# A fused attention and feed-forward kernel: two more batches of attention output turned by the DMA crossbar, and the last output group in two column halves

**Chip, cores, metric.** One core of one Trainium2 chip. The metric is the device time of one execution in microseconds (us).

## The reference

Block-causal attention over 8 batches, 8 heads, 576 positions, head size 64, then a feed-forward layer with a swish of slope beta on the 4608 rows:

```python
scores = 1/sqrt(64) * q @ k.T                  # (8, 8, 576, 576), keys of later 64-blocks masked
attn = softmax(scores)
x = (attn @ v) as rows (b, s), columns (h, d)  # 4608 x 512
h = x @ w_in                                   # 4608 x 2048
g = h / (1 + exp(-beta * h))
out = g @ w_out                                # 4608 x 512, float32
```

## The kernel before

The kernel is a list of operations that a planner in Python puts in order before the program is built. It imitates the engines and the DMA queue with fixed durations, and the outcome is one fixed order for each engine. In the program that is built each engine has its fixed list, with waits at semaphores between them. TensorE (PE) alternates between attention, in 32 units of two heads of a batch, and the feed-forward layer, in 9 row tiles of 512 rows (`w_in` on L740, `w_out` on L771).

SyncE (SP) only issues DMAs in this kernel. An issue is the time for which one DMA holds the queue; the DMA lands when its data has arrived. The queue issues the loads of q, k and v and all transposes by the DMA crossbar. From batch 2 on the crossbar turns q and k (QKT, one transpose of 2560 columns for two units). The attention output `xq` of a unit has to be turned too, into `xT`: up to batch XB - 1 on PE with a copy (nearly all by VectorE, DVE), from batch XB on by the crossbar:

```python
QB, XB, CAST = 2, 5, "POOL"
...
def pieces(b):                       # where batch b lies in xT, a ring of RX = 2560 columns
    z = []
    for t0, n in ((0, 512), (512, 64)):
        x0 = (S * b + t0) % RX
        m = min(n, RX - x0)
        z.append((t0, m, x0))
        if m < n:
            z.append((t0 + m, n - m, 0))
    return z
...
av = P.op("PE", 30 * 34, fav, deps=..., tiles=[te, Tv, pv, ti, tx], ...)   # values, L653; tx is an xq buffer, of two
...
if b >= XB:
    def fy(g, e, tx=tx, c=c, b=b):
        z = []
        for t0, n, x0 in pieces(b):
            ...                      # i: blocks of xq, m: 128 or the 64 of the last block
            z.append(g.dma_start_transpose(xT[:, c, x0:x0 + n].rearrange("c (t n) -> c t n", n=m), i))   # L685
        return z
    n = len(pieces(b))
    xt.append(P.op("SP", 400 + 300 * n + 700, fy, deps=nrm, tiles=[tx], xfer=1100, prio=-1, ...))
    continue
...                                  # else: five PE transposes (L697), DVE copies them to xT (L707)
```

The numbers in `P.op` are what the planner believes, in ns. The end of each row tile is four groups of 16 matmuls of 512 columns (in parts of four), each scaled by ScalarE (ACT, L782) into one of three `ost` buffers and stored (L788).

The softmax here doesn't subtract the row's maximum and nothing guards it: scores larger than these inputs give would overflow.

Of the kernel before, what the change touches and what calls it, by code (L numbers as in the profile page):

```python
# [4 lines left out]
ACT = mybir.ActivationFunctionType  # L5
ALU = mybir.AluOpType
# [7 lines left out]
DM = 512  # L14
NROWS = B * S
RC = 512
NRC = NROWS // RC
NJ = NF // 128
# [310 lines left out]
def bass_blockwise_causal_attn__then__act_swish_beta_kernel(  # L329
# [10 lines left out]
    with es:  # L340
        def sb(name, shape, dt):
            return es.enter_context(nc.sbuf_tensor(name, shape, dt))

        NQ = 2
        QB, XB, CAST = 2, 5, "POOL"
        NE = 3
        NS = 6
        RX = 5 * RC
# [16 lines left out]
        w_out = sb("w_out", [128, NJ, DM], bf16)  # L365
# [3 lines left out]
        gT = [sb(f"gT{i}", [128, NJ, RC], bf16) for i in range(2)]  # L369
        ost = [sb(f"ost{i}", [128, DM], f32) for i in range(3)]  # L370
        warm = sb("warm", [128, 2], f32)
        PS = es.enter_context(nc.psum_tensor("PS", [128, 8, 512], f32))
# [4 lines left out]
        P = Plan()  # L377
# [4 lines left out]
        def mm(n):  # L382
            return max(n / 2.4 + 3, 55.0)

        def act_t(n, ptr=0):
            return 0.833 * n + 93 + 93 * ptr

        def dve_t(n):
            return (n + 125) / 0.96

        LAG = 2
        def pr(u):
            b, c = divmod(u, NPAIR)
            return u if b < 1 else 10 * u if b < 2 else 994 + 100 * (b - LAG) + 4.9 * c

        def mk(fn):
            return lambda g, e: fn(g)
# [3 lines left out]
            out=identF[:], in_=identF[:], compare_op=ALU.not_equal, fill=1.0, base=0,  # L401
# [3 lines left out]
            out=identB[:], in_=identB[:], compare_op=ALU.not_equal, fill=1.0, base=0,  # L405
# [5 lines left out]
        for i in range(NQ):  # L411
# [3 lines left out]
            o = P.op("POOL", 200, mk(lambda g, i=i: g.memset(Vn[i][:, 4, :, 64:66], 0.0)), prio=-5)  # L415
# [6 lines left out]
        for i in range(NQ, NE):  # L422
# [8 lines left out]
                  deps=[bt, c2], tiles=[tb], lat=400, mode="full", prio=5)  # L431
        bC = P.op("DVE", dve_t(16), lambda g, e: g.tensor_scalar(
            out=beta[:], in0=PS[:, tb.slot, 0:NJ], scalar1=0.5, scalar2=None, op0=ALU.mult), deps=[bT], tiles=[tb])
# [3 lines left out]
        win, wout = [], []  # L437
# [15 lines left out]
        for i in range(NFILL):  # L453
# [10 lines left out]
            n = 215 if i < 16 else 110  # L464
            o = P.op("PE", n, ff, deps=[c2, c4], tiles=[tf], lat=n, mode="full", prio=1e6 + i)
# [6 lines left out]
        for b in range(B):  # L472
            ts, t = P.tile("Vs"), P.tile("V")
            tl[b] = t
            for h0, h1 in ([(0, 4), (4, 8)] if b == 0 else [(0, 8)]):
                vs = []
                for i in range(6):
# [8 lines left out]
                    n = (h1 - h0) / 8 * (1 if i < 4 else 0.25)  # L486
# [4 lines left out]
                n = (h1 - h0) / 8  # L491

                def fw(g, e, ts=ts, t=t, h0=h0, h1=h1):
                    return g.tensor_copy(Vn[t.slot][:, :, h0:h1, 0:64], Vs[ts.slot][:, :, h0:h1, :])  # L494

                o = P.op("POOL", 300 + 2140 * n, fw, deps=[*vs, *ones, *vzero], tiles=[ts, t],
                         prio=4 * b + 0.5 - (38.5 - 5 * (h0 > 0)) * (b < 1))
# [7 lines left out]
        def pieces(b):  # L505
# [8 lines that stand above are left out]
# [4 lines left out]
        for u in range(NU):  # L518
# [8 lines left out]
            if b < QB:  # L527

                turned = []
                for w, (nm, src) in enumerate((("Q", q), ("K", k))):  # L530
# [6 lines left out]
                    o = ld[nm, u] = P.op("SP", 420, fl, tiles=[ts], xfer=1050, prio=u, dma=["d_S", 0, 1])  # L537
                    o.pkt = 80.0

                    def fn(g, e, ts=ts, tn=tn, p=p, w=w):  # L540
# [4 lines left out]
                    o = P.op("POOL" if onp else "DVE", 850 if onp else 750, fn, deps=[o], tiles=[ts, tn],  # L545
                             prio=-40 + 3 * u if onp else -1)

                    def ft(g, e, tn=tn, pt=pt, p=p, w=w):
                        for i in range(6):
# [4 lines left out]
                    o = P.op("PE", 6 * 43, ft, deps=[o, c4], tiles=[tn, pt, tt_], lat=6 * 43 + 170, mode="full",  # L554
                             prio=pr(u))
# [6 lines left out]
            elif p == 0:  # L562

                for w, (nm, src) in enumerate((("Q", q), ("K", k))):
                    ts = P.tile("ST")

                    def fl(g, e, ts=ts, src=src, b=b, c=c):
# [3 lines left out]
                             for i in range(4)]  # L571
# [4 lines left out]
                    o = ld[nm, u] = ld[nm, u + 1] = P.op("SP", 5 * 600, fl, deps=szero, tiles=[ts], xfer=3200, prio=u,  # L576
                                                         dma=["d_S5", 0, 5])
# [17 lines left out]
            for g0 in range(4):  # L595
                ps = P.tile("PP" if g0 < 3 else "P1")

                def fq(g, e, ps=ps, g0=g0, tqk=tqk, p=p):
                    blocks = {0: [(0, 0, 512, 0)], 1: [(1, 128, 576, 0), (0, 512, 576, 448)],
                              2: [(2, 256, 576, 0), (3, 384, 576, 320)], 3: [(4, 512, 576, 0)]}[g0]  # L600
                    for t, q0, q1, off in blocks:
                        m = min(128, 576 - 128 * t)
                        for h in range(2):
# [9 lines left out]
                o = P.op("PE", 220 if g0 < 3 else 60, fq, deps=cps, tiles=[ps, tqk] + [te] * (b > 0),  # L613
                         lat=(220 if g0 < 3 else 60) + 200, mode="row", prio=pr(u) + .1 + .1*(g0 >= 2))
                if g0 < 3:
# [3 lines left out]
                    x = P.op("ACT", act_t(1024), fe, deps=[o], tiles=[ps, te], lat=act_t(1024) + 93, prio=0)  # L619
# [7 lines left out]
                else:  # L627
                    def fe(g, e, ps=ps, te=te):
                        return g.activation(E4[te.slot][:], PS[:, ps.slot, 0:64], ACT.Exp, scale=0.125)  # L629
                    x = P.op("ACT", act_t(64), fe, deps=[o], tiles=[ps, te], lat=act_t(64) + 93, prio=0)  # L630
# [17 lines left out]
            def fav(g, e, te=te, pv=pv, Tv=Tv, c=c):  # L648
                for h in range(2):
                    for i in range(5):  # L650
# [7 lines left out]
                      lat=30 * 34 + 180, mode="full", prio=pr(u)+.4 + 5 * (b < 1))  # L658
# [8 lines left out]
            r = P.op("DVE", 150, fr, deps=[av], tiles=[pv, ti], prio=0)  # L667
# [9 lines left out]
            if b >= XB:  # L677
# [10 lines left out]
                n = len(pieces(b))  # L688
# [40 lines left out]
        for r in range(NRC):  # L729
            row = RC * r  # L730
            b0, b1 = row // S, (row + RC - 1) // S
            xd = [xt[4 * b + c] for b in range(b0, b1 + 1) for c in range(4)]
            tg = P.tile("gT")
            gs, hs = [], []
            for j in range(NJ):
                ph, tt = P.tile("P1"), P.tile("th")

                def fh(g, e, ph=ph, j=j, row=row):
                    for c in range(4):
                        z = g.matmul(PS[:, ph.slot, :], w_in[:, c, 128 * j:128 * j + 128], xT[:, c, row % RX:row % RX + RC],  # L740
                                     start=(c == 0), stop=(c == 3))
                    return z

                o = P.op("PE", 4 * mm(512), fh, deps=xd + [win[j // 4]], tiles=[ph, tg], lat=4 * mm(512) + 170,
                         mode="full", prio=1000 + 100 * r + j)

                hs.append(o)

                def fs(g, e, ph=ph, tt=tt, j=j):
                    return g.activation(th[tt.slot][:], PS[:, ph.slot, :], ACT.Tanh, scale=beta[:, j:j + 1])  # L750
                a = P.op("ACT", act_t(512, 1), fs, deps=[o, bC], tiles=[ph, tt], lat=act_t(512, 1) + 93, prio=0)

                def fg(g, e, ph=ph, tt=tt, tg=tg, j=j):
                    return g.scalar_tensor_tensor(out=gT[tg.slot][:, j, :], in0=th[tt.slot][:], scalar=1.0,  # L754
                                                  in1=PS[:, ph.slot, :], op0=ALU.add, op1=ALU.mult)
                gs.append(P.op("DVE", dve_t(512), fg, deps=[a], tiles=[ph, tt, tg], prio=0))

            for b in range(B):
                if any((S * b + a) // RC - RX // RC == r for a in (0, S - 1)):
                    for c in range(4):  # L760
                        xt[4 * b + c].deps += hs
            for w in range(4):
                po, to = P.tile("P1"), P.tile("ost")


                parts = [(4 * a, 4 * a + 4) for a in range(4)]
                o = None
                for j0, j1 in parts:
                    def fo(g, e, po=po, tg=tg, w=w, j0=j0, j1=j1):
                        for j in range(j0, j1):  # L770
                            z = g.matmul(PS[:, po.slot, :], gT[tg.slot][:, j, 128 * w:128 * w + 128], w_out[:, j, :],  # L771
                                         start=(j == 0), stop=(j == NJ - 1))
                        return z

                    n = j1 - j0
                    o = P.op("PE", n * mm(512), fo, deps=gs[j0:j1] + wout[j0 // 4:(j1 + 3) // 4] + ([o] if o else []),
                             tiles=[po, tg], lat=n * mm(512) + 170, mode="full",
                             prio=1000 + 100 * r + 16 + (w + 0.01 * j0 if r or w > 2 else 0.01 * j0 + 0.001 * w))

                def fv2(g, e, po=po, to=to):  # L780
                    if e == "ACT":
                        return g.activation(ost[to.slot][:], PS[:, po.slot, :], ACT.Copy, scale=0.5)  # L782
                    return g.tensor_scalar(out=ost[to.slot][:], in0=PS[:, po.slot, :], scalar1=0.5, scalar2=None,
                                           op0=ALU.mult)
                x = P.op("ACT", 600, fv2, deps=[o], tiles=[po, to], lat=680, prio=0)

                def fd(g, e, to=to, row=row, w=w):
                    return [g.dma_start(out[row + 128 * w:row + 128 * w + 128, :], ost[to.slot][:])]  # L788
                P.op("ACT", 500, fd, deps=[x], tiles=[to], xfer=900, dma=["d_ost", to], prio=-1)

        P.schedule()
# [69 lines left out]
```

## Time and profile before

| | before |
|---|---|
| time, median of 4 runs | 354.8 us (353.98 to 356.67) |
| span of the profiled run | 353.9 us |
| PE, end of the last matmul | 350.5 us |
| PE transposes of xq (L697) / xT transposes on SP (L685) | 100 / 24 |
| PE wait for QKT landings | 0.5 us |

The profiled run is one execution, and its span is about 1.8 us under its time. The prediction starts from 355.6 us, the median of three runs. SP's share is not on the page, since issues are not counted as busy.

### The profile page before, as it was taken

How to read it: one execution, taken by the hardware profiler on the slowest of the kernel's cores; microseconds unless marked ns; L12 is line 12 of the kernel's file. 1: busy time of each engine (PE TensorE's matmuls, PEld its weight loads, DVE VectorE, ACT ScalarE, POOL GpSimd, SP SyncE). 2: the span in 40 equal slices, each digit the busy share in tenths (PEclk: the TensorE clock that was granted, in tenths of full speed). 3: DMA queues.
4: the chain of work that ended last, by engine and by line, in shares of the span. 5: the costliest groups of instructions: out<-in, count | busy, mean ns of one | idle time of the engine just before them, and what ended most of it. 6: DMA issues, size and time to landing. Idle time of an engine off the chain costs nothing.

```text
span 353.9 us, 6788 instructions
## 1 busy us (share of the span) xinstructions
PE 337.4 (95%) x2734; PEld 168.4 (48%) x2779; DVE 163.6 (46%) x367; ACT 212.0 (60%) x314; POOL 76.3 (22%) x105
## 2 busy tenths in 40 slices
PE   7897999999999999999999999999999999999996
PEld 4473455444455445545544445444444444444442
DVE  4665785055434664227821474137704703802810
ACT  2945973269376797189772976298616715814821
POOL 6476071214044053053013310500000000000000
PEclk9998999999999999999999999999999999999999
DMA  7999999999999999998489986861111011011002
GB/s 209 188 243 231 185 186 200 238 212 193 209 251 204 211 212 203 225 250 167 85 189 166 220 175 143 199 138 36 32 63 59 0 61 59 0 61 59 1 31 89
DMA packets 146528, 52.05 MB, mean 147 GB/s; under 512 B 134704, under 2 KB 141888, under 8 KB 146496
## 3 DMA queue, kind: packets, MB, share of 16 engines
q1 hardware_dynamic: 137088, 37.97, 53.8%
q10 hardware_dynamic: 5184, 9.44, 8.1%
q0 software_dynamic: 4224, 4.19, 7.3%
q8 instruction: 22, 0.36, 0.4%
q14 instruction: 10, 0.08, 0.1%
HBM read 36.71 MB, written 9.44 MB: 130 GB/s over the span
## 4 chain that ended last, share of the span: by engine, by line
PE 75%; SPq 7%; DMA 6%; ACT 5%; issue 3%; DVE 2%; POOL 1%; ACTq 0%; POOLq 0%
PE PS L771 31%; PE PS L740 30%; PE PS L609 6%; PE PS L653 5%; DMA w_in<-in_moe_w_in_dram 3%; ACT E L617 2%; DMA QKT<-QKn 2%; ACT th L750 2%; SPq L480 2%; SPq L685 2%; PE PS L697 2%; SPq L483 2%; DVE gT L754 2%; SPq L569 1%; DMA Vs<-in_v_dram 1%
## 5 line engine op out<-in xcount | busy, mean ns | idle before, releaser
L740 PE MATMUL PS<-xT,w_in 128*128 128x512 bf16 x552 | 129.8, 381 | 5.5 <-DMA w_in<-in_moe_w_in_dram 2.3
L754 DVE SCALAR_TENSOR_TENSOR gT<-th,PS 128x512 bf16<-128x512 f32 x144 | 97.5, 684 | 79.2 <-ACT th L750 78.5
L771 PE MATMUL PS<-w_out,gT 128*128 128x512 bf16 x555 | 128.6, 379 | 2.4 <-issue 1.9
L617 ACT ACTIVATE E<-PS 128x1024 bf16<-128x1024 f32 x96 | 95.9, 1041 | 29.9 <-PE PS L609 29.7
L750 ACT ACTIVATE th<-PS,beta 128x512 f32<-128x512 f32 x144 | 98.1, 706 | 26.3 <-PE PS L740 25.5
L740 PEld LDWEIGHTS PS<-xT,w_in 128*128 128x128 bf16 x576 | 53.1, 98 | 67.3 <-issue 5.1
L771 PEld LDWEIGHTS PS<-w_out,gT 128*128 128x128 bf16 x576 | 53.3, 98 | 64.3 <-issue 4.1
L782 ACT ACTIVATE ost<-PS 128x512 f32<-128x512 f32 x36 | 21.7, 603 | 75.4 <-PE PS L771 75.4
L580 POOL CAST QKn<-ST 128x640 bf16<-128x640 f32 x48 | 34.7, 722 | 55.6 <-DMA ST<-in_k_dram 29.6
L609 PE MATMUL PS<-QKT 64*64 64x64 bf16 (+5 forms) x384 | 38.8, 283 | 1.1 <-DMA QKT<-QKn 0.5
L653 PEld LDWEIGHTS PS<-Vn,E 128*128 128x128 bf16 x960 | 32.6, 97 | 6.2 <-ACT E L629 0.3
L494 POOL CAST Vn<-Vs 128x2560 bf16<-128x2560 f32 (+1 forms) x9 | 18.8, 2088 | 77.2 <-DMA Vs<-in_v_dram 69.5
L653 PE MATMUL PS<-Vn,E 128*128 128x65 bf16 x960 | 33.9, 193 | 0.0
L623 DVE MEMSET E<- 64x64 uint32 x64 | 7.2, 112 | 49.7 <-ACT E L617 48.3
L609 PEld LDWEIGHTS PS<-QKT 64*128 64x128 bf16 (+1 forms) x384 | 13.3, 96 | 28.9 <-issue 10.9
L672 DVE TENSOR_TENSOR xq<-PS,inv 128x640 bf16<-128x640 f32 x32 | 26.3, 823 | 0.8
L707 DVE COPY xT<-PS 128x64 bf16<-128x64 bf16 (+2 forms) x40 | 9.6, 287 | 9.6 <-PE PS L697 9.5
L558 DVE COPY QKT<-PS 128x576 bf16<-128x576 bf16 x16 | 12.0, 756 | 4.5 <-PE PS L550 4.2
L665 DVE RECIPROCAL inv<-PS 128x10 f32<-128x10 f32 x32 | 7.0, 218 | 14.1 <-PE PS L653 13.9
L541 POOL CAST QKn<-ST 96x768 bf16<-96x768 f32 x14 | 11.8, 845 | 6.4 <-DMA ST<-in_k_dram 3.4
L625 DVE MEMSET E<- 64x128 uint32 x32 | 5.3, 165 | 13.6 <-ACT E L617 12.3
L697 PE MATMUL PS<-identB,xq 128*128 128x128 bf16 (+1 forms) x100 | 10.5, 216 | 0.5 <-DVE xq L672 0.3
(33 smaller groups left out, 57.9 us busy)
## 6 DMA issues: line engine op xcount, KB each, us to landing
out_dram<-ost ACTq DMA_DIRECT2D x36, 256.0 KB, 2.5
Vs<-in_v_dram SPq DMA_DIRECT2D x28, 256.0 KB, 4.1
ST<-in_q_dram SPq DMA_DIRECT2D x48, 128.0 KB, 3.2
ST<-in_k_dram SPq DMA_DIRECT2D x48, 128.0 KB, 3.2
ST<-in_q_dram SPq DMA_DIRECT2D x8, 288.0 KB, 6.2
ST<-in_k_dram SPq DMA_DIRECT2D x8, 288.0 KB, 6.8
w_in<-in_moe_w_in_dram POOLq DMA_DIRECT2D x4, 512.0 KB, 14.8
w_out<-in_moe_w_out_dram POOLq DMA_DIRECT2D x4, 512.0 KB, 10.6
```

The costliest lines, as they stand in the source:

```text
L494: return g.tensor_copy(Vn[t.slot][:, :, h0:h1, 0:64], Vs[ts.slot][:, :, h0:h1, :])
L580: return g.tensor_copy(QKn[tn.slot][:].rearrange("p a w n -> p (a w n)")[:, 640 * (2 * a + w):][:, 0:640] .rearrange("p (t h d) -> p t h d ...
L609: z = g.matmul(o, QKT[tqk.slot][r, p, 1, 128 * t:128 * t + m], QKT[tqk.slot][r, p, 0, q0:q1])
L617: return g.activation(E3[te.slot][:, g0, :, :], PS[:, ps.slot:ps.slot + 2, :], ACT.Exp, scale=0.125)
L653: z = g.matmul(o, eblk(te, t, i, h), Vn[Tv.slot][:, t, 2 * c + h, 0:65], start=(t == 0), stop=(t == i))
L672: return g.tensor_tensor(xq[tx.slot][:].rearrange("p i (h d) -> p h i d", h=2), both(pv, 0, 64), x, ALU.mult)
L697: z = g.transpose(PSb[:, px.slot, 128 * i:128 * i + r], xq[tx.slot][0:r, i, :], identB[0:r, 0:r])
L740: z = g.matmul(PS[:, ph.slot, :], w_in[:, c, 128 * j:128 * j + 128], xT[:, c, row % RX:row % RX + RC], start=(c == 0), stop=(c == 3))
L750: return g.activation(th[tt.slot][:], PS[:, ph.slot, :], ACT.Tanh, scale=beta[:, j:j + 1])
L754: return g.scalar_tensor_tensor(out=gT[tg.slot][:, j, :], in0=th[tt.slot][:], scalar=1.0, in1=PS[:, ph.slot, :], op0=ALU.add, op1=ALU.mult)
L771: z = g.matmul(PS[:, po.slot, :], gT[tg.slot][:, j, 128 * w:128 * w + 128], w_out[:, j, :], start=(j == 0), stop=(j == NJ - 1))
L782: return g.activation(ost[to.slot][:], PS[:, po.slot, :], ACT.Copy, scale=0.5)
```

## The change

The intent is to take 40 transposes off PE, the engine that is busy all the time, and to shorten the end: the last of the 36 groups becomes two of 256 columns, so that the last scaling and the last store are of half the size.

```diff
-        QB, XB, CAST = 2, 5, "POOL"
+        QB, XB, CAST = 2, 3, "POOL"
...
-            for w in range(4):
+            for w, d0, d1 in [(w, 0, DM) for w in range(4 if r < NRC - 1 else 3)] + (
+                    [] if r < NRC - 1 else [(3, 0, DM // 2), (3, DM // 2, DM)]):
...
-                            z = g.matmul(PS[:, po.slot, :], gT[tg.slot][:, j, 128 * w:128 * w + 128], w_out[:, j, :],
+                            z = g.matmul(PS[:, po.slot, 0:d1 - d0], gT[tg.slot][:, j, 128 * w:128 * w + 128],
+                                         w_out[:, j, d0:d1], start=(j == 0), stop=(j == NJ - 1))
...                                  # durations, scaling and store in the same way with d0 and d1
```

More of the change, by code (lines that the diff above doesn't have):

```diff
@@ L768, in bass_blockwise_causal_attn__then__act_swish_beta_kernel, with fo @@
                 for j0, j1 in parts:
-                    def fo(g, e, po=po, tg=tg, w=w, j0=j0, j1=j1):
+                    def fo(g, e, po=po, tg=tg, w=w, j0=j0, j1=j1, d0=d0, d1=d1):
                         for j in range(j0, j1):
-                            z = g.matmul(PS[:, po.slot, :], gT[tg.slot][:, j, 128 * w:128 * w + 128], w_out[:, j, :],
-                                         start=(j == 0), stop=(j == NJ - 1))
-                        return z
-                    n = j1 - j0
@@ L776, in bass_blockwise_causal_attn__then__act_swish_beta_kernel @@
-                    o = P.op("PE", n * mm(512), fo, deps=gs[j0:j1] + wout[j0 // 4:(j1 + 3) // 4] + ([o] if o else []),
-                             tiles=[po, tg], lat=n * mm(512) + 170, mode="full",
-                             prio=1000 + 100 * r + 16 + (w + 0.01 * j0 if r or w > 2 else 0.01 * j0 + 0.001 * w))
-                def fv2(g, e, po=po, to=to):
-                    if e == "ACT":
-                        return g.activation(ost[to.slot][:], PS[:, po.slot, :], ACT.Copy, scale=0.5)
-                    return g.tensor_scalar(out=ost[to.slot][:], in0=PS[:, po.slot, :], scalar1=0.5, scalar2=None,
-                                           op0=ALU.mult)
@@ L785, in bass_blockwise_causal_attn__then__act_swish_beta_kernel @@
-                x = P.op("ACT", 600, fv2, deps=[o], tiles=[po, to], lat=680, prio=0)
-                def fd(g, e, to=to, row=row, w=w):
-                    return [g.dma_start(out[row + 128 * w:row + 128 * w + 128, :], ost[to.slot][:])]
+                            z = g.matmul(PS[:, po.slot, 0:d1 - d0], gT[tg.slot][:, j, 128 * w:128 * w + 128],
+                                         w_out[:, j, d0:d1], start=(j == 0), stop=(j == NJ - 1))
+                        return z
+                    n = (j1 - j0) * mm(d1 - d0)
@@ new lines, in bass_blockwise_causal_attn__then__act_swish_beta_kernel, with fv2 @@
+                    o = P.op("PE", n, fo, deps=gs[j0:j1] + wout[j0 // 4:(j1 + 3) // 4] + ([o] if o else []),
+                             tiles=[po, tg], lat=n + 170, mode="full",
+                             prio=1000 + 100 * r + 16 + (w + 0.01 * j0 + 0.3 * (d0 > 0) if r or w > 2 else
+                                                         0.01 * j0 + 0.001 * w))
+                def fv2(g, e, po=po, to=to, n=d1 - d0):
+                    if e == "ACT":
+                        return g.activation(ost[to.slot][:, 0:n], PS[:, po.slot, 0:n], ACT.Copy, scale=0.5)
+                    return g.tensor_scalar(out=ost[to.slot][:, 0:n], in0=PS[:, po.slot, 0:n], scalar1=0.5,
+                                           scalar2=None, op0=ALU.mult)
@@ L789, in bass_blockwise_causal_attn__then__act_swish_beta_kernel, with fd @@
+                x = P.op("ACT", act_t(d1 - d0) + 80, fv2, deps=[o], tiles=[po, to], lat=act_t(d1 - d0) + 160, prio=0)
+                def fd(g, e, to=to, row=row, w=w, d0=d0, d1=d1):
+                    return [g.dma_start(out[row + 128 * w:row + 128 * w + 128, d0:d1], ost[to.slot][:, 0:d1 - d0])]
                 P.op("ACT", 500, fd, deps=[x], tiles=[to], xfer=900, dma=["d_ost", to], prio=-1)
```

## The prediction

> **What bounds the kernel now.** I read the page first: engine shares, the row of slices, the chain that ended last.
>
> ```profile
> PE 337.4 (95%) x2734; PEld 168.4 (48%) x2779; DVE 163.6 (46%) x367; ACT 212.0 (60%) x314; POOL 76.3 (22%) x105
> ...
> PE   7897999999999999999999999999999999999996
> ...
> DMA  7999999999999999998489986861111011011002
> ...
> PE 75%; SPq 7%; DMA 6%; ACT 5%; issue 3%; DVE 2%; POOL 1%; ACTq 0%; POOLq 0%
> ```
>
> PE is busy in every slice, so the matmul stream in its fixed program order sets the time, and what shortens that stream is worth its full length. But the DMA row is full until about 155 us, and 7% of the chain is SP's queue, which issues all loads and all crossbar transposes. So next I read SP's own timeline. An excerpt (start, length, line, operation, tile):
>
> ```profile
> 197.56 2.31 SPq L569 DMA_DIRECT2D ST<-in_k_dram  x4
> 199.91 0.60 SPq L572 DMA_DIRECT2D ST<-in_k_dram  x1
> 200.56 4.11 SPq L587 DMA_TRANSPOSE QKT<-QKn  x1
> 204.72 1.21 SPq L480 DMA_DIRECT2D Vs<-in_v_dram  x2
> 205.97 3.00 SPq L685 DMA_TRANSPOSE xT<-xq  x2
> 209.01 3.14 SPq L587 DMA_TRANSPOSE QKT<-QKn  x1
> 212.19 2.77 SPq L685 DMA_TRANSPOSE xT<-xq  x2
> ```
>
> Each record begins some 0.05 us after the last ended. From 91 to 233 us SP pauses noticeably only once, from 165.5 to 169.5, where it waits for the first attention output of batch 5. It is as full as PE, and the page's engine shares do not show it, because issues are not counted as busy there. The third view, the chain in order of time, shows how close this comes to PE:
>
> ```profile
> 230.24 8.18 DMA QKT<-QKn
> 238.42 0.14 issue
> 238.56 0.22 PE PS L609 x2
> ```
>
> The last of twelve QKT transposes (batch 7, second pair of head pairs) lands at 238.4, and PE begins to use it at 238.56. The list of waits gives 0.5 us of PE time for it, the only wait of the kind. I set each QKT landing from 91 us on beside the first scores matmul of its pair: they are early by 5.8, 7.5, 8.4, 8.7, 9.3, 10.9, 11.5, 2.5, 15.6 and 0.1 us. So SP keeps up with PE, and no more.
>
> **What the Trainium skill says.** "Perfetto Trace Analysis", section "What 'DMA-bound' means", lists as one form that the issuing engine's track is solid with DMA slices, which are descriptor generation. That is SP here. Its section "Per-instruction lifecycle" (the part on HWDGE) says that such a record starts when the semaphores are satisfied and does not hold the data movement; the trace agrees: an xT transpose is 1.23 us long and lands 2.5 us after its issue. "DMA: Bandwidth & Descriptors", section "Issuing engines are not separate DMA queues", calls the issue time usually small beside the transfer; this trace differs, since an xT transpose holds the queue for half its time to landing. "TensorE: Matmul & The Clock Gate", section "Back-to-back issue gap", gives 518 cycles for 512 columns and 262 for 256; the trace has four L740 matmuls in 0.86 us, 216 ns each, and agrees on the first. Nothing in the trace has an isolated stream of 256 warm columns; I take 108 ns, half of 216.
>
> **The change part by part.** Part one concerns batches 3 and 4, eight units (a unit is two heads of a batch).
>
> ```profile
> L697 PE MATMUL PS<-identB,xq 128*128 128x128 bf16 (+1 forms) x100 | 10.5, 216 | 0.5 <-DVE xq L672 0.3
> L707 DVE COPY xT<-PS 128x64 bf16<-128x64 bf16 (+2 forms) x40 | 9.6, 287 | 9.6 <-PE PS L697 9.5
> ...
> xT<-xq SPq DMA_TRANSPOSE x24, 2.5
> ```
>
> Removed from PE: five transposes a unit, 40 of the 100. By the start of the next operation in PE's timeline the eight groups took 0.45, 0.45, 0.33, 0.34, 0.46, 0.45, 0.34 and 0.34 us, 3.2 us together, all on the path. Removed from DVE: copies of 0.52 us (batch 3) and 0.59 us (batch 4), 4.4 us, beside an engine with half its time idle: counted as nothing.
>
> Added to SP: batch 3 lies in xT in two pieces, batch 4 in three because the ring of 2560 columns wraps in it, so 4 x 2 + 4 x 3 = 20 transposes at 1.23 us, 24.6 us, all between 112 and about 175 us and all ahead of the last QKT. Not all becomes delay. The pause of 4.0 us disappears. And issues between 91 and 165.5 us are longer than the shortest of their line: summed over 48 q and k issues, 12 short ones, 15 of v and 6 QKT transposes, 11.9 us over the minimum. I take that for pressure from the full DMA engines, of which a slower stream of loads gives back between nothing and all; I take half. 24.6 - 4.0 - 6.0 = 14.6 us later at the last QKT. Its landing took 8.2 us against a median of 5.8; with a less crowded queue I take 2.7 us off: 11.9.
>
> Against it stands the order of PE, which the kernel's own planner makes anew. It charges each unit's transposes 1.1 us of transfer, 8.8 us for eight units, and may move the later attention back behind row-tile work by up to that. Before the change batches 6 and 7 stand at the places that their priorities give (row tiles 4 and 5 begin at 195 and 232 us, batches 6 and 7 at 194 and 230), so part of the shift will be caught up: I take 4.4, half. PE, in order, can do nothing else at a late QKT, so at the last one it is 11.9 - 4.4 = 7.5 us later than now on net, the 3.2 us saved being consumed there (gross waiting 10.7 us).
>
> Part two is the end. ACT's timeline:
>
> ```profile
> 349.68 0.60 ACT L782 ACTIVATE ost<-PS 128x512 f32<-128x512 f32 x1 [5.24 <-PE PS L771]
> 350.31 0.34 ACTq L788 DMA_DIRECT2D out_dram<-ost  x1
> 350.75 0.60 ACT L782 ACTIVATE ost<-PS 128x512 f32<-128x512 f32 x1 [0.47 <-PE PS L771]
> 351.38 0.34 ACTq L788 DMA_DIRECT2D out_dram<-ost  x1
> ```
>
> PE ends at 350.50, yet the last scaling starts at 350.75, since ACT is still on the tile before: the last two row tiles alternate on PE in parts of four matmuls and end 0.86 us apart. With halves, the last one's 16 matmuls (1.73 us at 108 ns) should stand alone at the end, so ACT is free: 0.25 us. A scaling of 256 columns is shorter by 256 x (1041 - 603)/512 = 0.22 us, from the means for 1024 and 512 columns. A store of half the size lands perhaps 0.2 us sooner (an estimate from 2.5 us median and 2.0 shortest). PE does 32 matmuls of 108 for 16 of 216: no change. The third output buffer is free again, as the first tiles' stores left at 343. Sum: 0.6 us saved.
>
> **The sum.** +7.5 - 0.6 = +6.9 us over 355.6: 362.5.
>
> **The rivals.** First: the transposes are hidden, PE meets no late QKT, and only 3.2 + 0.6 us remain as gain: 351.8. For it: the landings are 8 to 11 us early in the stretch where SP gets most of its work, the planner knows of the load, and the kernel has been tuned. Against it: the landing 0.1 us before use. It needs nearly all of the 11.9 us back as well as the planner's full shift. Second: SP's work is delay in full, 24.6 - 4.0 = 20.6 us with little shift: 355.6 + 20.6 - 0.6 - 2 = about 373. For it: queue records shrink only from 0.58 to 0.55 us a load between the crowded stretch and the one after 169. Third: an attention output waits in one of only two xq buffers behind a late queue, DVE then blocks on the next, and with it the gT products that PE needs. Outputs of the same buffer are 10 to 15 us apart, so with the queue ten late this is close, and would add 2 to 5 us. In batch 6 the third unit's output was done at 217.7 and its transposes issued at 224.9 without a wait of DVE in the list.
>
> **Range and chances.** I give the late queue 60%, with 355 to 370 around 362.5, the hidden case 40%, around 352: 0.6 x 362.5 + 0.4 x 351.8 = 358.2; I take 358.5. Range 351 to 368. Faster by over 2% means under 348.5 us, for which PE would have to save twice what is on it: 4%. Slower by over 2% means over 362.7: 40%. Within 2%: 56%.
>
> **What would show it.** In the changed profile: 60 PE transposes left on the line of L697 and 44 xT transposes on SP; SP solid from 91 us until the last QKT issue, and that issue near 245 us rather than 230; scores matmuls waiting on QKT landings for about 10 us in all, at the later pairs of batches 4 to 6 first; PE's busy time down by 3 us while its idle time rises; at the end about 2.8 us from PE's last matmul to the end of the span, against 3.4. If PE shows no wait on QKT, the first rival holds and the time is near 352. If the QKT waits are small but DVE waits for xT landings, it is the third. I would be wrong altogether if PE's order changed so that attention of the last batches stands far later, behind whole row tiles.

## The result

The changed kernel takes 370.3 us (median of 4 runs, 369.87 to 373.28) against 354.8: a ratio of 1.045 (95% interval 1.038 to 1.052), slower by 4.5%. Here and below a ratio is the mean time of one kernel's fast runs over that of the other's of the same rounds, so not quite the ratio of the medians.

The page of the changed kernel, the same rows as in the prediction:

```profile
PE 341.4 (93%) x2711; PEld 169.7 (46%) x2755; DVE 160.7 (44%) x347; ACT 211.8 (58%) x315; POOL 76.0 (21%) x105
...
PE   7997999999999999978788998599999999999997
...
DMA  8999999999999987785779676986412003003003
...
PE 65%; DMA 9%; SPq 9%; ACT 8%; DVE 4%; issue 3%; POOL 0%
```

PE now has holes between 40% and 65% of the span, and the shares of SP's queue and the DMAs in the chain have grown. The list of waits of the changed kernel (engine, tile and line <- what it waited for: us in total, times, longest) names them:

```profile
PE PS L609 <- DMA QKT<-QKn: 8.0, 3, 5.0
PE PS L653 <- DMA xT<-xq: 3.5, 2, 3.4
```

In the kernel before, the same list has one such line:

```profile
PE PS L609 <- DMA QKT<-QKn: 0.5, 1, 0.5
```

The longest of the waits in the changed kernel, in the chain in order of time (start, length, what):

```profile
223.73 2.99 DMA ST<-in_k_dram
...
226.77 0.21 POOL QKn L580
226.99 7.25 DMA QKT<-QKn
234.24 0.05 issue
234.29 1.28 PE PS L609 x10
```

The tenth QKT transpose (batch 6, second pair) is issued at 227.0, lands at 234.24, and PE goes on at 234.29 after 5.0 us of waiting. Before, the same transpose was issued at 200.56 and used at 209.16. SP's timeline of the changed kernel ahead of it is solid:

```profile
214.91 2.56 SPq L685 DMA_TRANSPOSE xT<-xq  x2
217.51 2.46 SPq L569 DMA_DIRECT2D ST<-in_q_dram  x4
220.02 0.65 SPq L572 DMA_DIRECT2D ST<-in_q_dram  x1
220.71 2.98 SPq L569 DMA_DIRECT2D ST<-in_k_dram  x4
223.73 0.61 SPq L572 DMA_DIRECT2D ST<-in_k_dram  x1
224.38 2.56 SPq L685 DMA_TRANSPOSE xT<-xq  x2
226.99 4.27 SPq L587 DMA_TRANSPOSE QKT<-QKn  x1
```

Second, the granted clock, the share of TensorE's full clock that its throttle lets through. Busy time by stretch (length, PE, PEld for its weight loads, DVE, ACT, POOL, then granted TensorE clock, DMA share, GB/s):

```profile
180.00:190.00 10.00, 6.43 (x49) 3.53 (x48) 1.04 (x2) 1.19 (x2) 2.41 (x4) 0.83 0.57 136
...
230.00:240.00 10.00, 5.38 (x23) 1.58 (x24) 0.39 (x3) 3.20 (x5) 0.00 (x0) 0.66 0.98 204
240.00:250.00 10.00, 9.68 (x110) 5.01 (x111) 3.39 (x10) 7.93 (x12) 2.32 (x1) 1.00 0.83 186
```

The clock records show it at half speed from 185.4 to 188.8 and from 233.2 to 240.0 us, at the two longest waits. The kernel before has no half clock there. Both have an early stretch near 30 us, 6.8 us long here and 3.4 before. I do not count that to the change: it is missing in the profiles of experiments 1 and 2, and 6.8 us long again in that of 5.

**Where the time went.** PE's last matmul ends at 365.70 in place of 350.51, 15.2 us later. At the tenth QKT PE is 234.29 - 209.16 = 25.1 us later. From there to its last matmul it needs 131.4 us, before 141.35: of these 131.4, (240.0 - 234.3)/2 = 2.85 us are lost to half clock, so 141.35 - 128.55 = 12.8 us of matmuls have been moved ahead of this place by the planner. 25.1 - 12.8 + 2.85 = 15.2. The end gives 0.8 us back.

The end did what it was meant to. ACT's timeline of the changed kernel:

```profile
363.55 0.87 ACT L785 ACTIVATE ost<-PS 128x512 f32<-128x512 f32 x2 [3.96 <-PE PS L773]
364.18 0.82 ACTq L791 DMA_DIRECT2D out_dram<-ost  x2
365.73 0.38 ACT L785 ACTIVATE ost<-PS 128x256 f32<-128x256 f32 x1 [1.31 <-PE PS L773]
366.15 0.34 ACTq L791 DMA_DIRECT2D out_dram<-ost  x1
```

The last scaling begins 0.03 us after PE's end (before, 0.24) and takes 0.38 us in place of 0.60; from PE's end to the end of the span it is 2.62 us, before 3.38.

### The profile page after: what moved, and what is told of

Same layout as the page of the kernel before. It is cut to its first block, busy times and chain, and to the rows that moved or that the text cites. A ratio compares the mean times of both kernels' runs of the same rounds, so it can differ in the third digit from the quotient of the medians.

```text
span 368.3 us, 6750 instructions
## 1 busy us (share of the span) xinstructions
PE 341.4 (93%) x2711; PEld 169.7 (46%) x2755; DVE 160.7 (44%) x347; ACT 211.8 (58%) x315; POOL 76.0 (21%) x105
## 4 chain that ended last, share of the span: by engine, by line
PE 65%; DMA 9%; SPq 9%; ACT 8%; DVE 4%; issue 3%; POOL 0%
PE PS L773 29%; PE PS L740 26%; PE PS L609 5%; PE PS L653 4%; ACT E L617 4%; ACT th L750 4%; DMA QKT<-QKn 3%; DVE gT L754 3%; SPq L569 3%; DMA w_in<-in_moe_w_in_dram 3%; DMA ST<-in_k_dram 3%; SPq L685 2%; SPq L480 2%; SPq L483 1%; DVE xq L672 1%
## 5 line engine op out<-in xcount | busy, mean ns | idle before, releaser
L740 PE MATMUL PS<-xT,w_in 128*128 128x512 bf16 x553 | 132.3, 383 | 4.8 <-DMA w_in<-in_moe_w_in_dram 1.8
L773 PE MATMUL PS<-w_out,gT 128*128 128x512 bf16 (+1 forms) x571 | 131.8, 378 | 2.5 <-issue 2.0
L773 PEld LDWEIGHTS PS<-w_out,gT 128*128 128x128 bf16 x592 | 55.4, 99 | 64.3 <-issue 6.8
L785 ACT ACTIVATE ost<-PS 128x512 f32<-128x512 f32 (+1 forms) x37 | 21.7, 591 | 76.4 <-PE PS L773 76.3
L609 PE MATMUL PS<-QKT 64*64 64x64 bf16 (+5 forms) x384 | 39.5, 289 | 9.0 <-DMA QKT<-QKn 8.0
L609 PEld LDWEIGHTS PS<-QKT 64*128 64x128 bf16 (+1 forms) x384 | 13.3, 97 | 41.2 <-issue 11.6
L459 PE MATMUL PS<-identF,identB 128*128 128x256 bf16 x36 | 7.1, 353 | 2.6 <-POOL identF L400 2.4
L629 ACT ACTIVATE E<-PS 128x64 bf16<-128x64 f32 x32 | 6.2, 244 | 3.1 <-PE PS L609 1.8
```

The lines of the kernel that those rows point to most:

```text
L609: z = g.matmul(o, QKT[tqk.slot][r, p, 1, 128 * t:128 * t + m], QKT[tqk.slot][r, p, 0, q0:q1])
L740: z = g.matmul(PS[:, ph.slot, :], w_in[:, c, 128 * j:128 * j + 128], xT[:, c, row % RX:row % RX + RC], start=(c == 0), stop=(c == 3))
L773: z = g.matmul(PS[:, po.slot, 0:d1 - d0], gT[tg.slot][:, j, 128 * w:128 * w + 128], w_out[:, j, d0:d1], start=(j == 0), stop=(j == NJ - 1))
L785: return g.activation(ost[to.slot][:, 0:n], PS[:, po.slot, 0:n], ACT.Copy, scale=0.5)
```

## The experiments

**Theory.** SP's queue is full from 65 us until the last QKT with the time that issues take, whatever they move. Twenty more issues make QKT late, and PE, in fixed order, waits. **Rivals.** (a) The crossbar's traffic loads the DMA engines, and not the issue time. (b) Two xq buffers are too few behind the queue: PE's values matmul claims one, so PE itself waits. (c) The planner, which believes an xT issue to be cheap, puts attention too early; in another order the loss would not be there. (d) The halves have a part.

**1 and 2. Each part alone.** The halves with XB = 5, and XB = 3 with the last tile whole.

> The last row tile in halves alone; the attention output stays on TensorE up to batch 4. Both theories (late SP queue, loaded DMA engines) say nothing here changes SP: time 0.4 to 0.8 us under the kernel before, no QKT wait over 1 us, about 2.6 us from the end of the last matmul to the end of the span. A rise of over 2 us would mean that the halves, by the new order that the planner makes, have a part in the loss.

> The crossbar from batch 3 on alone, the last row tile whole. If the halves have no part in the loss: 370 to 372 us, PE waiting 10 to 15 us on QKT and xT landings and one or two stretches of half clock. If the loss comes from both together: under 366.

Measured: the halves alone 354.3 us, ratio 0.997 (0.993 to 1.002); the interval does not tell it from no change. In its trace the stretch after PE's last matmul is 2.59 us against 3.38. XB = 3 alone: 372.3 us, ratio 1.050 (1.044 to 1.055), with PE waits of 8.3 us on QKT and 3.6 on xT. So (d) falls: the loss is all in the crossbar part.

**3. Same order, fewer issues.** The changed kernel with one transpose of 640 columns for a unit in place of one of 512 and one of 64. The 64 columns too many lie where the next batch writes afterwards, and waits were added for that. The planner is given the same durations, and the order of PE, ACT, DVE and POOL was compared and is the same, instruction for instruction.

```diff
-                    for t0, n, x0 in pieces(b):
-                        ...          # 512 columns, then 64
+                    for t0, n, x0 in wide(b):   # 640 columns; two pieces for batch 4 alone
+                        i = xq[tx.slot][:, t0 // 128:(t0 + n) // 128, :].rearrange("p t n -> p (t n)")
+                        z.append(g.dma_start_transpose(xT[:, c, x0:x0 + n].rearrange("c (t n) -> c t n", n=128), i))
...
-                n = len(pieces(b))
+                n = len(wide(b))
+                if b > XB:
+                    nrm = nrm + [xt[4 * (b - 1) + c]]
```

> The changed kernel with the order of all instructions kept, but each unit's transpose of 512 columns and of 64 columns made one of 640 (two for batch 4, where the ring wraps): 24 xT issues in place of 44, the crossbar moves slightly more data than in the changed kernel. If SP's issue time is the cause (20 issues of 1.25 us, 25 us): QKT landings about 20 us earlier from batch 5 on, PE waits on QKT and xT under 2 us in all, no half clock after 40 us, time 352 to 355. If the load on the DMA engines or the crossbar itself is the cause: time stays at 367 to 371.

Measured: 354.8 us, ratio 0.997 (0.991 to 1.002). The number of xT issues fell from 44 to 24, the orders of the other engines stayed, and the whole loss is gone. The crossbar turned slightly more columns than in the changed kernel, so (a) falls. The QKT landings of batches 5 to 7 came 5 to 16 us earlier than in the changed kernel, not the 20 us that I expected. The last one is still 9.1 us later than in the kernel before (247.48 against 238.42): the order that the planner made for the changed kernel leaves room for that much, and not for the 24.4 us of the changed kernel. One wait is left, in the list of waits of this run:

```profile
PE PS L614 <- DMA QKT<-QKn: 1.7, 1, 1.7
```

(L614 is the scores line, L609 in the kernel before; added lines move the numbers, here and below.) The wait is at the eighth QKT (landed 187.06), and 3.4 us of half clock follow it, against my expectation of none; with it the 3.2 us saved on PE do not show in the time.

**4. Same order, more issues that move nothing.** The kernel before, with five tiny crossbar transposes of a constant ahead of each of four QKT transposes. The order of the other engines was compared with the kernel before and is the same; SP's differs by the twenty alone.

```diff
+                nd = 5 if b in (4, 5) else 0
                 def ft(g, e, tn=tn, td=tt_, nd=nd, k=u // 2 % 2):
-                    return [g.dma_start_transpose(QKT...)]
+                    return [g.dma_start_transpose(xD[:, k, 64 * i:64 * i + 64], identB[0:64, :])
+                            for i in range(nd)] + [g.dma_start_transpose(QKT...)]
```

> The kernel before with the order of all its instructions kept, and ahead of four QKT transposes (batch 4 and 5) five tiny crossbar transposes each, 64 columns of the identity into a tile that nobody reads: 20 more issues on SP, hardly any data. If SP's issue time is the cause: last QKT issue 18 to 25 us later than 230, PE waits of 15 to 22 us on QKT, half clock after the long ones, time 372 to 380. If engine load is the cause, or if SP could give the time back: 354 to 358.

Measured: 376.2 us, ratio 1.057 (1.051 to 1.063). One of the four runs was slow; the ratio leaves it out, and the median of the other three is 375.4 us. From SP's timeline of this run, and its list of PE's waits:

```profile
113.32 1.22 SPq L481 DMA_DIRECT2D Vs<-in_v_dram  x2
114.64 7.17 SPq L591 DMA_TRANSPOSE xD<-identB  x5
121.85 3.12 SPq L592 DMA_TRANSPOSE QKT<-QKn  x1
```

```profile
PE PS L617 <- DMA QKT<-QKn: 13.1, 4, 4.3
```

An issue of 64 columns takes 1.18 to 2.05 us, mean 1.36, no less than the xT transposes of 512 and 64 columns in the kernel before (mean 1.29). The last QKT issue is at 250.2 in place of 230.2: 20 us late for 27.2 us of issues. PE's waits of 13.1 us are under the 15 to 22 us that I expected. Between the third and the last QKT issue 3.1 us came back from pauses, the one of 4 us among them, and 4.0 us on balance from the other issues (QKT transposes 3.37 us in place of 3.69, v loads 0.71 in place of 0.82, but q and k loads 0.61 in place of 0.58). The kernel lost about 21 us by issues that carry next to nothing, without any new order. With experiment 3 this settles the cause: the loss can be made and removed by the number of crossbar issues on SP alone. Both experiments vary crossbar issues, so it stays open whether the 1.3 us of an issue is SP's own work or a fixed cost of a transpose for which SP is held up.

**5. A third xq buffer in the changed kernel** (`range(2)` to `range(3)` and its slots).

> The changed kernel with three xq buffers in place of two. If the shortage of these buffers is the main cause (the third rival of the prediction): time near 355. If the late SP queue is the cause: only the 3.4 us wait of the values matmuls for an xT landing goes (and the half clock after it), the QKT waits stay or grow by as much since PE only arrives earlier at them, time 366 to 370.

Measured: 368.8 us, ratio 1.035 (1.029 to 1.042). The planner, which knows of the buffer, made a new order. The waits for xT landings are gone; in their place the waits on QKT have grown from 8.0 to 10.5 us, as if PE only came to them earlier. So (b) is real as a wait but not the main cause: the kernel still loses 12.6 us, and behind the same late queue one wait takes the other's place. Whether the third buffer gains anything is open, since the intervals of the two ratios overlap.

```profile
PE PS L609 <- DMA QKT<-QKn: 10.5, 3, 5.0
```

**6 and 7. The planner told the truth.** The changed kernel with SP's durations as the traces show them; then the same with the third xq buffer.

```diff
-xt.append(P.op("SP", 400 + 300 * n + 700, fy, ...
+xt.append(P.op("SP", 1300 * n, fy, ...
-turned = [P.op("SP", 1500, ft, ...
+turned = [P.op("SP", 3700, ft, ...
```

> The changed kernel, but its planner is told what SP's issues took in the traces: 1.3 us for each xT transpose and 3.7 us for a QKT transpose, in place of 0.85 to 0.67 and 1.5. SP has the same 44 xT issues. If the loss is only that PE's fixed order comes to the late QKT too soon, the planner now puts row-tile work ahead of the attention of batches 5 to 7 and the waits go: PE waits on QKT under 3 us, time 352 to 357. If a late SP queue must cost this time in any order: 366 or more.

> The changed kernel with 44 xT issues, but the planner told the issue times and three xq buffers: what is left of the loss when both of its helpers are mended and only SP's length stays. The xT waits of 4.4 us of the told kernel go; QKT waits stay at 3 to 6 us: 358 to 363. If 353 or less, SP's length alone costs nothing once the order fits.

Measured: told alone 364.8 us, ratio 1.025 (1.019 to 1.030); with the third buffer 362.7 us, ratio 1.018 (1.012 to 1.024). The first missed what I expected of it on either side. Its waits fell to 3.9 us on QKT and 4.4 on xT, and two stretches of half clock stayed; the second came in at 358 to 363 as expected, but still waits 6.9 us on QKT. The medians lie 8.6 and 7.1 us over those of the kernel before in the same rounds, against 15.5 for the changed kernel. So (c) is a part: a better order, with the buffer or without, recovers about half, and the other half stayed with SP's 44 issues. Only the two durations were mended; the planner's transfer time of 1.1 us for a unit was left, and a fully true plan was not tried.

**8. A part of SP's work on another queue.** The changed kernel with the v loads of batches 3 to 7 issued from ACT's queue.

```diff
-vs.append(P.op("SP", 300 + 550 * n, fv, ..., dma=["d_V", h0, 1]))
+vs.append(P.op("ACT" if b >= 3 else "SP", 360 if b >= 3 else 300 + 550 * n, fv, ...,
+               dma=["d_VA" if b >= 3 else "d_V", h0, 1]))
```

> The changed kernel with the loads of v for batches 3 to 7 issued from the ACT queue, so SP loses 30 issues of about 0.75 us (22 us) and keeps the 44 xT transposes; all bytes stay. If SP's issue time is the cause: QKT landings some 15 us earlier at the end, waits under 4 us, time 352 to 358. If the crossbar's transposes or the loaded engines are: 366 or more.

Measured: 371.1 us, ratio 1.040 (1.035 to 1.046), a miss. SP has pauses now (thirteen over 0.3 us from 91 us to the last QKT issue, 31 us in all), so it is no longer full, and yet QKT is late. From the list of waits of all engines in this run (POOL is GpSimd; the list puts down one wait to the semaphore that came last):

```profile
POOL QKn L580 <- DMA ST<-in_k_dram: 69.0, 11, 13.3
...
PE PS L609 <- DMA QKT<-QKn: 15.6, 6, 5.3
```

ACT issues a v load only between its own activations, one to ten us apart (112.6, 114.3, 123.8, 125.6, 129.5 and 133.0 us for one batch). POOL casts v in its fixed order ahead of the next q and k and stands until the last v has landed, at 135.9; the casts that QKT needs come after that, and SP then waits for them. By what I had written the time speaks for the rival. But the relief turned one wait into another, and the planner made a new order too, so I take the run as no test of the theory. That the v loads are what held POOL is read from the trace, not tested.

**9. Half of it: the crossbar from batch 4 on** (XB = 4 in the changed kernel).

> The changed kernel with the crossbar from batch 4 on: 12 more xT issues than before (about 15 us) in place of 20. If a late SP queue is the cause, the loss is not in proportion: the pause of 4 us and the earliness of 8 to 11 us of batches 5 and 6 take the first part of it. 15 - 4 = 11 us late, less what the planner moves ahead (13 us in the changed kernel): waits of 0 to 6 us, time 354 to 361. If crossbar load is the cause: 12/20 of the loss, 363 to 365.

Measured: 363.8 us, ratio 1.023 (1.017 to 1.029), outside what I expected of the theory and inside what I had written for crossbar load. Experiments 3 and 4 had by then ruled the load out, so my sum was wrong, and the trace shows where. The last QKT issue came 16.1 us later than in the kernel before (246.3 against 230.2), and not 11, and the earliness of batches 5 and 6 did not swallow it. PE waited 3.9 us on QKT and 3.3 us on xT landings, and half clock of 6.8 us in two stretches (3.4 lost) followed. I had put no term for either the xq buffers or the clock. Against the 0.5 us of QKT waits before, and with 1.6 us of PE transposes and 0.8 at the end taken off: 3.9 - 0.5 + 3.3 + 3.4 - 1.6 - 0.8 = 7.7; the medians differ by 8.2.

**10, 11 and 12. A better version.** One transpose for a unit (as in 3), a told planner (as in 6), three xq buffers, the halves; with the crossbar from batch 3, and as controls from batch 5 and from batch 2.

> A try at a better version: batch 3 on over the crossbar with one transpose per unit (24 xT issues), planner told the issue times, three xq buffers, halves at the end. By the SP theory nothing is late, so PE keeps the 3.2 us and the end its 0.7: 350.5 to 352.5, no QKT wait over 1 us.

> Control for the better version: the same one transpose per unit, told planner, three buffers and halves, but batches 3 and 4 stay on TensorE. The eight units' PE transposes are worth 3.2 us where SP is not late, so this should be 2 to 4 us slower than the better version with the crossbar from batch 3: ratio to the kernel before 0.995 to 1.003.

> The better version with the crossbar from batch 2 on: four more units off PE (1.7 us), four more issues on SP (5 us). SP is full from 65 us on, so the gain may be eaten: 0 to 1.5 us under the version from batch 3, ratio to the kernel before 0.985 to 0.993; over 0.995 if SP is late again.

Measured: from batch 3 353.3 us, ratio 0.993 (0.988 to 0.998); from batch 5 354.4 us, 0.996 (0.992 to 1.001); from batch 2 354.7 us, 0.999 (0.994 to 1.005). All three missed something: the first is over its 350.5 to 352.5 us, the control is about 1 us slower than it and not 2 to 4, and the version from batch 2 is over its 0.993. The version from batch 3 beats both kernels, that before by 0.7% and the changed one by about 5% (by the ratios to the kernel before, in different rounds). It differs from experiment 3 in the told planner and the third buffer, which were not tried there one by one. In its trace PE's last matmul ends at 347.99, against 350.51 before, and PE waits 1.0 us on QKT in all, with no half clock after 34 us. The three intervals overlap, so which batch is best is not settled. The trace of the version from batch 5 shows the last QKT 7.8 us early in place of 0.1: SP has room there that PE cannot use. That from batch 2 waits again, 1.4 us on the eighth QKT, though with no half clock.

## Why the prediction was wrong

- **What bounds the kernel.** Right. PE and SP were both full, and SP's fullness, which the page hides, decides (experiments 3 and 4).
- **PE's saving, 3.2 us.** The 40 transposes are gone from PE (60 left). By the sum of PE's own losses it holds: waits over 0.3 us rose from 7.1 to 19.0 us, half clock by (17.1 - 3.4)/2 = 6.8 us (1.7 of it from the early stretch, which is not the change's), and 11.9 + 6.8 - 3.2 = 15.5 against 15.2 measured. As a gain of time it is not settled: in the version from batch 3 PE's last matmul ends 2.7 us earlier than in its control from batch 5 (one profile each), but the intervals of their times overlap.
- **"24.6 - 4.0 - 6.0 = 14.6 us later at the last QKT".** This is the step that failed: how much of SP's added work becomes delay. The last QKT issue came at 257.9 in place of 230.2, 27.6 us later, 13 us more than predicted. Each term has its part. The work: 22 xT transposes more stood ahead of it, not 20, at a mean of 1.30 us, and took 28.1 us; the 1.23 us of the prediction is the median of the kernel before, whose mean is 1.29. The pause: the one of 4.0 us went as foreseen, but two new ones of about 1 us came at 242 and 254, and pauses gave back 1.4 us in all. The give-back, the largest miss: of the 6.0 us nothing came, and the other issues took 2.0 us more. Between the third and the tenth QKT issue the q and k loads were 0.58 us each before and 0.60 after, those of v 0.83 and 0.86, the QKT transposes 3.70 and 3.68. With the third QKT issue 1.0 us earlier this is 28.1 - 1.4 + 2.0 - 1.0, or 27.6 after rounding. Why the length over the minimum did not shrink is open; in experiment 4 some 4 us of it did come back.
- **The landing, 2.7 us sooner.** The last one took 4.95 us in place of 8.2, 3.2 sooner; but it was no longer the place that counts. The tenth was, whose landing took 7.25 us, before 6.1.
- **"I take 4.4, half" for the planner's shift.** Too small as well, an error in the other direction: 12.8 us were moved ahead, more even than the 8.8 us that I set as the most. The 8.8 us are a misreading of the kernel: beside the transfer of 1.1 us the planner books `400 + 300 * n + 700` ns of SP's time for each unit, 1.7 us in batch 3 and 2.0 in batch 4, 14.8 us in all. That this is why it moved 12.8 is argued and not tested. Experiment 4, which kept the order and added twenty issues, lost 21 us.
- **The net at the late QKT, 7.5 us.** 25.1 - 12.8 = 12.3 at the tenth QKT, and 2.85 of half clock on it make 15.2, in place of 7.5. The clock was not in my sum at all. "TensorE: Matmul & The Clock Gate", section "Why this matters for your kernels", advises against PE idle gaps of over about 3 us for this reason; in the changed kernel the waits of 3.4 and 5.0 us were each followed by half clock.
- **The end, 0.6 us.** Right, and a little small: 3.38 to 2.62 us, so 0.8.
- **The rivals.** The second rival, SP's work as delay in full, "about 373", was near the measured 370.3; it was described and then given no weight in the range, although I had written that the queue's records shrink only a little, which was evidence for it. That its number came so near is partly luck: it had the queue 20.6 us late, about 2 us of shift and no clock, and the trace has 27.6, 12.8 and the half clock. The third rival came as waits of PE and not of DVE: the values matmul claims the xq buffer, so PE stood 3.4 us for an xT landing. Experiment 5 shows that it cost little on its own. The first rival, to which I gave 40%, had for it the tuning of the kernel, the planner's knowledge of the load, and that the landings were early in the stretch where SP gets its work; the landing that was 0.1 us early showed that there was nothing to spare at the end.

## What to carry to other kernels

An engine that only issues DMAs can be the second bound of a kernel without standing in the table of engine shares: ask for its timeline, and set each landing beside its first use. In these runs moving work from a full engine to a full queue cost time where it added twenty issues, and one transpose for a unit in place of two made the same move free. When a queue is full, count most of the added issue time as delay (27.6 us for 28.1 in the changed kernel, 20 us for 27 in experiment 4), add the clock that waits of a few us cost, and give the unpleasant rival its share of the range.

## What the Trainium skill lacked or had wrong

- "DMA: Bandwidth & Descriptors", section "DMA Transpose (X-bar)", has no issue time, and the page's only such times for a transpose stand in a table on trn3, under "previous generations", for other forms. In these runs an issue on SP took 1.18 to 2.05 us for 64 columns (mean 1.36), 1.29 on average for the xT transposes of 512 and of 64 columns together, and 3.1 to 5.7 us for 2560 in the kernel before.
- The same page, section "Issuing engines are not separate DMA queues", calls the issue time usually small beside the transfer. Here it was half of the time to landing (1.23 of 2.5 us), and twenty issues that moved next to nothing cost about 21 us.
- "TensorE: Matmul & The Clock Gate", section "Why this matters for your kernels", puts the gap that costs the clock at over about 3 us. Waits of 2.5, 2.6 and 2.8 us were followed by half clock here too (experiments 5 and 6), and a wait of 1.7 us in experiment 3; one of 2.4 us in experiment 2 was not. So no clean limit shows. Half clock came in stretches of 3.4 us or twice that.
- The same page, section "Back-to-back issue gap", names 131 ns for each matmul of 512 columns in a real stream. Here it was 216 ns (four in 0.86 us), as its formula for isolated ones has it; for 256 columns 19 spacings took 2.07 us at the end of the changed kernel, 109 ns each, which agrees with its 262 cycles.
